# Dense 128-row projection of K, Q and attention outputs, with SBUF to SBUF moves between layouts, and norm products on GpSimd

## Chip, cores, metric

One core of a Trainium2 chip. The metric is device time in microseconds (us) from the first to the last instruction of one execution, as median over several executions. Ratios and their 95% intervals are computed from the mean time of one kernel's fast runs over the mean of the other's in the same rounds, so they are not quite the ratio of the medians that are quoted beside them.

## The reference

```python
# x: (1, 2048, 640) bf16, both branches read A_x; H = 32 heads of 20, D = 640
g = sigmoid((x * gate_w).sum(-1))                   # per token
a = full_attention(x, A_wqkv, A_wo)                 # softmax(q k^T / sqrt(20)) v, all 2048 keys
b = sliding_attention(x, B_wqkv, B_wo)              # 8 keys at distance 0, 2, ..., 14
out = g * a + (1 - g) * b                           # each branch through its own 640x640 output matrix
```

Branch A has 32 x 2048 x 2048 exponentials. That is over a million columns of 128 elements, and they decide the time of this kernel.

## The kernel before

The program is planned when it is built. A small scheduler in Python (`T(engine, duration, function, reads, writes)`) knows an estimated duration for each operation. It lets generators ("K projection", "Q projection", "B branch") compete for PSUM banks and for gaps on the engines, and writes out one fixed instruction order per engine, with the semaphore waits that the named buffers need. Every engine then works through its own list in order. An estimate that is wrong does not make the kernel wrong, only badly ordered. And any edit re-plans everything behind it, so small differences between two variants need not come from the edit itself.

The main loop works in tiles of two or three units. A unit is 128 keys x 512 queries of one head: a score matmul on TensorE (PE), an exponential on ScalarE (ACT), and a value matmul. A tile is three units wide only if the third bank of its score buffer is not lent to side work at that moment.

```python
# score buffers of three banks each; their third banks are lent to side work
score = [ps(1536, "score0"), ps(1536, "score1")]
BANKS = [(sbank, 0), (score[0], 1024), (score[1], 1024)]
# ... cut ...
def exp(s):                                   # one ScalarE instruction for 2 or 3 units
    exps[s] = T("act", actc(512 * n), lambda e: e.activation(
        ebuf[s % NE][:, 0:512 * n], score[s % 2][:, 0:512 * n], ACTF.Exp, scale=LN2 / STEP), ...)
```

Some units go to VectorE (DVE) instead: one operation from PSUM (`uD`), then, for a quad of four such units, five shifted integer operations (`eD`) whose sum in the value matmul approximates the exponential. The scheduler sends a quad this way whenever it sees VectorE idle.

Heads are handled in "quads": four heads of 20 rows, each padded to 32 partitions, so that four heads fill 128 partitions. Before the change every projection is made straight into this padded layout, which wastes 48 of 128 rows:

```python
def gen_k(q):                                 # 7 quads, 4 token chunks each (the first quad is made apart)
    T("dve", 0.36, w_pad(kvw, WKP_OFF, stage, 4 * DH * q, D, q), ...)        # pad the weights
    for tcc in range(4):
        b = yield from bank()
        # 5 matmuls into side[b]; then
        T("dve", dvc(512), ... kT[:, q, ...] = side[b] + onesrow ...)
        T("dve", dvc(512), ... tensor_reduce(kmx4, max, absolute) ...)       # bound for the softmax

def gen_q(g):                                 # one per group: (512 queries) x (quad)
    # 5 matmuls; qabs = |q| on DVE; a matmul with KM subtracts the bound; qT = scaled on DVE
    sl = g % 2                                # two Q buffers
# ... cut ...
def gen_norm(g):                              # after the last value matmul of a group
    T("dve", ... transpose(oTt, obank)); T("dve", ... reciprocal); T("dve", ... times gate)
    T("dve", dvc(512), lambda e: e.tensor_tensor(oo, ii, ib, ALU.mult), ...)
    T("dve", dvc(512), lambda e: e.transpose(oTn[:, sl, :], oNt), ...)
# ... cut ...
# output projection: 5 matmul groups of branch B and 8 of branch A (one per padded quad)
mms += [(side[b][:, 0:c1 - c0], oTn[:, (qc * NQ + q) % NSLOT, tok], woA_r[:, q, c0:c1]) for q in range(NQ)]
```

## Time and profile before

| | before |
|---|---|
| time, median of the first runs | 927.16 us (926.71 to 927.2) |
| span of the profiled execution | 924.7 us |
| ScalarE busy | 881.4 us, of it exponentials 863.5 |
| exponentials on ScalarE | 829 instructions, 1856 units |
| units on the VectorE path | 192 (48 quads) |

First some lines of the page. The first line gives for each engine its busy time, the share of the span and the number of instructions. Each digit of a row below is the busy share of one fortieth of the span in tenths; PEclk is the granted TensorE clock in tenths.

```profile
PE 905.5 (98%) x13935; PEld 322.1 (35%) x13938; DVE 697.6 (75%) x1209; ACT 881.4 (95%) x864; POOL 27.2 (3%) x23
...
ACT  6999999996999999999999999999999999999996
...
PEclk9999999998999999999999999999999999999999
```

ScalarE is full except for the head, the tail and one hole near 220 us, where the clock dips as well. PE's 98% does not mean that PE is the limit. The scheduler fills PE's gaps with dummy matmuls that keep the clock up: 392 groups of four, begun about 0.215 us apart where they follow each other in this trace.

The groups view with shapes kept apart shows: line, engine, operation, out<-in, shapes, count | busy us, mean ns of one | idle time before it, and what ended it.

```profile
L1239 ACT ACTIVATE ebuf<-score 128x1024 bf16<-128x1024 f32 x631 | 607.9, 1037 | 23.1 <-PE score L1216 20.0 <-ACT ebuf L1239 0.2
...
L1239 ACT ACTIVATE ebuf<-score 128x1536 bf16<-128x1536 f32 x198 | 282.4, 1469 | 3.9 <-PE score L1216 3.2
...
L594 DVE TENSOR_SCALAR eD<-uD 128x2048 int16<-128x2048 uint16 x240 | 164.1, 715 | 17.7 <-PE obank L1274 16.5
L1229 DVE TENSOR_SCALAR uD<-score 128x512 uint16<-128x512 f32 x192 | 131.7, 688 | 80.4 <-PE score L1216 79.2
...
L608 POOL COPY kvw<-stage 128x640 bf16<-128x640 bf16 x15 | 23.4, 1560 | 194.8 <-PE score L456 194.0
```

Two-unit exponentials dominate, 631 against 198. From the two mean times, a unit costs about 0.43 us and an instruction 0.17 us on top. But neighbouring instructions overlap (the two rows add up to more than the 863.5 us of the group without shapes): back to back, they start 0.92 and 1.34 us apart on average in this trace, which leaves about 0.08 us per instruction. So width is worth something.

The stage table gives for each stretch (us): its length, then busy time and instruction count of PE, PEld (weight loads), DVE, ACT and POOL (GpSimd), the granted clock, the DMA share and GB/s.

```profile
0.00:69.00 69.00, 65.58 (x861) 26.59 (x863) 43.27 (x100) 59.18 (x60) 3.79 (x8) 1.00 0.32 90
69.00:231.00 162.00, 155.78 (x2144) 48.05 (x2147) 131.87 (x217) 150.43 (x146) 23.40 (x15) 0.98 0.13 22
231.00:902.00 671.00, 666.10 (x10541) 239.41 (x10533) 516.60 (x883) 657.95 (x649) 0.00 (x0) 1.00 0.07 9
902.00:924.70 22.70, 18.09 (x401) 8.08 (x402) 5.92 (x10) 13.84 (x13) 0.00 (x0) 0.98 0.09 31
```

The number to subtract is ACT from the length: ScalarE idles 9.8, 11.6, 13.1 and 8.9 us in the four stages, 43.3 us in all.

Two single lines were used in the prediction. The first is the eD group between 200 and 232 us, while GpSimd copies B's weights. The second, from the listing of the tile WqP, gives the time that SyncE (SP) takes to issue a load: minimum/median/maximum in ns.

```profile
L594 DVE TENSOR_SCALAR eD<-uD 128x2048 int16<-128x2048 uint16 x10 | 13.6, 1398 | 1.2 <-PE obank L1274 1.2
```

```profile
L498 SPq DMA_DIRECT2D WqP<-in_A_wqkv_dram x150: 367/505/2952, 22.2 to 839.0; - x150
```

Last, GpSimd's two padding copies in the head, which the first K and Q projections wait for (timeline: start, duration):

```profile
5.67 0.52 POOL L425 COPY kvw<-repB 128x400 bf16<-128x400 bf16 x1 [2.30 <-DMA repB<-in_A_wqkv_dram]
8.01 0.53 POOL L425 COPY WqP<-repB 128x400 bf16<-128x400 bf16 x1 [1.83 <-DMA repB<-in_A_wqkv_dram]
```

### The profile page before, as it was taken

The numbers are of one execution on the slowest core, as the hardware profiler recorded it, in microseconds if no ns is written. First come the engines' busy times: TensorE is split into PE (matmuls) and PEld (weight loads), VectorE is DVE, ScalarE is ACT, GpSimd is POOL, SyncE is SP. The second block draws the span as 40 slices with busy tenths as digits, with TensorE's granted clock in tenths as the row PEclk, the third lists the DMA queues.
The fourth block names the chain that finished last, engine by engine and source line by source line (L and its number), as shares of the span: only waits on it lengthen the run. The fifth ranks groups of instructions, "written<-read, shape, count | busy, mean of one in ns | idle before, by whom it ended". The sixth has DMA issues, their size and how long they took to land.

```text
span 924.7 us, 31431 instructions
## 1 busy us (share of the span) xinstructions
PE 905.5 (98%) x13935; PEld 322.1 (35%) x13938; DVE 697.6 (75%) x1209; ACT 881.4 (95%) x864; POOL 27.2 (3%) x23
## 2 busy tenths in 40 slices
PE   8999999998999999999999999999999999999997
PEld 4333332322343333333433433433333343332333
DVE  6567778888888787988777877787786778678552
ACT  6999999996999999999999999999999999999996
POOL 1000000027000000000000000000000000000000
PEclk9999999998999999999999999999999999999999
DMA  6111000030000011001101001100001110000000
GB/s 194 25 50 16 6 3 7 6 113 6 3 7 6 7 14 14 3 6 14 15 6 14 10 7 14 14 7 7 3 7 13 21 14 7 2 6 7 2 2 30
DMA packets 89027, 16.27 MB, mean 18 GB/s; under 512 B 81596, under 2 KB 88252, under 8 KB 88892
## 3 DMA queue, kind: packets, MB, share of 16 engines
q1 hardware_dynamic: 88892, 14.27, 9.5%
q8 instruction: 110, 1.80, 0.8%
q14 instruction: 25, 0.20, 0.1%
HBM read 11.63 MB, written 2.62 MB: 15 GB/s over the span
## 4 chain that ended last, share of the span: by engine, by line
PE 82%; ACT 12%; DVE 2%; issue 2%; DVEq 0%; ACTq 0%
PE score L1216 25%; PE obank L1274 18%; PE score L456 16%; PE side L456 12%; ACT ebuf L1239 12%; PE side L1295 3%; PE obank L1295 3%; DVE eD L594 1%; PE score L1295 1%; PE score L669 1%; PE side L669 0%; PE obank L366 0%; PE score L945 0%; PE side L724 0%; PE score L724 0%
## 5 line engine op out<-in xcount | busy, mean ns | idle before, releaser
L1239 ACT ACTIVATE ebuf<-score 128x1024 bf16<-128x1024 f32 (+1 forms) x829 | 863.5, 1140 | 27.0 <-PE score L1216 23.2
L1216 PE MATMUL score<-qT,kT 32*128 32x512 bf16 x2048 | 332.5, 385 | 4.8 <-ACT ebuf L1239 2.4
L1229 DVE TENSOR_SCALAR uD<-score 128x512 uint16<-128x512 f32 x192 | 131.7, 688 | 80.4 <-PE score L1216 79.2
L1216 PEld LDWEIGHTS score<-qT,kT 32*128 32x128 bf16 x2048 | 80.0, 91 | 285.1 <-ACT ebuf L1239 143.6
L1274 PE MATMUL obank<-ebuf,vA 128*21 128x512 bf16 x1856 | 175.3, 386 | 3.8 <-DVE eD L594 2.8
L594 DVE TENSOR_SCALAR eD<-uD 128x2048 int16<-128x2048 uint16 x240 | 164.1, 715 | 17.7 <-PE obank L1274 16.5
L456 PE MATMUL score<-xT,kvw 128*32 128x256 bf16 (+1 forms) x1780 | 87.2, 299 | 0.8 <-ACT ebuf L1239 0.6
L1274 PE MATMUL obank<-eD,vA 128*21 128x512 bf16 x960 | 76.3, 380 | 0.0
L1274 PEld LDWEIGHTS obank<-ebuf,vA 128*21 128x21 bf16 x1856 | 43.1, 89 | 92.6 <-issue 68.2
L1295 PE MATMUL side<-xT,ident 128*32 128x512 bf16 x772 | 57.3, 382 | 0.0
L456 PE MATMUL side<-xT,kvw 128*32 128x256 bf16 (+1 forms) x1180 | 54.6, 289 | 0.2 <-DVE qT L519 0.2
L736 DVE TENSOR_TENSOR stage<-vB,repB 128x1280 bf16<-128x1280 bf16 x64 | 51.1, 816 | 0.3
L456 PEld LDWEIGHTS score<-xT,kvw 128*32 128x32 bf16 x1780 | 40.6, 95 | 30.4 <-issue 19.0
L659 DVE TENSOR_TENSOR stage<-qB,kB 128x1280 bf16<-128x1280 bf16 x64 | 50.1, 817 | 0.1
L1295 PE MATMUL obank<-xT,zero 128*32 128x512 bf16 x568 | 46.3, 384 | 0.0
L566 DVE STREAM_TRANSPOSE oTt<-obank 128x512 f32<-128x512 f32 x32 | 22.8, 714 | 16.1 <-PE obank L1274 15.9
L456 PEld LDWEIGHTS side<-xT,kvw 128*32 128x32 bf16 x1180 | 27.6, 96 | 17.3 <-issue 10.6
L1274 PEld LDWEIGHTS obank<-eD,vA 128*21 128x21 bf16 x960 | 23.8, 92 | 16.6 <-issue 1.9
L608 POOL COPY kvw<-stage 128x640 bf16<-128x640 bf16 x15 | 23.4, 1560 | 194.8 <-PE score L456 194.0
L456 PE MATMUL score<-xT,WqP 128*32 128x512 bf16 x300 | 25.0, 396 | 2.9 <-DVE uD L1229 2.9
L456 PE MATMUL side<-stage,ident 128*32 128x512 bf16 (+1 forms) x352 | 26.8, 372 | 0.0
L456 PE MATMUL score<-woA_r,oTn 128*32 128x128 bf16 (+1 forms) x568 | 26.7, 290 | 0.0
(165 smaller groups left out, 725.7 us busy)
## 6 DMA issues: line engine op xcount, KB each, us to landing
WqP<-in_A_wqkv_dram SPq DMA_DIRECT2D x150, 20.0 KB, 2.3
stage<-in_B_wqkv_dram SPq DMA_DIRECT2D x1, 2400.0 KB, 9.4
out_dram<-outsb SPq DMA_DIRECT2D x12, 160.0 KB, 1.8
oTn<-in_A_x_dram SPq DMA_DIRECT2D x2, 640.0 KB, 5.1
kvw<-in_A_wqkv_dram SPq DMA_DIRECT2D x1, 800.0 KB, 8.7
stage<-in_A_wqkv_dram SPq DMA_DIRECT2D x1, 800.0 KB, 9.8
woA_r<-in_A_wo_dram SPq DMA_DIRECT2D x4, 200.0 KB
woBp<-in_B_wo_dram SPq DMA_DIRECT2D x5, 160.0 KB
```

Source lines behind the costliest of these rows:

```text
L456: ins = e.matmul(o[32 * j:32 * j + 32, :], l[:, 32 * j:32 * j + 32], r, start=(first and i == 0), stop=(last and i == n - 1), skip_group_c ...
L566: T("dve", dvc(512), lambda e: e.transpose(oTt[:, :], obank[:, :]), reads=["obank"], writes=["oTt"])
L594: T("dve", 0.11 + 0.1334 * n, lambda e, k=k, sl=sl: e.tensor_scalar(eD[:, sl % NS, 0:512 * n].bitcast(I16), uD[d % 2][:, 0:512 * n], 0.25, ...
L608: T("pool", 2.2, lambda e, o=o, i=i: e.tensor_copy(o, i), reads=["stage"], writes=[("WkP", qq) for qq in range(NQ)] + ["WvA", ("wBp", m)])
L659: TB(dvc(CN * TOK, 2), lambda e, w=w, ks=ks: e.tensor_tensor(prodB(w), qB[:, :, :], ks, ALU.mult), reads=["qB", "kB"], writes=[("prod", w) ...
L669: ins = e.matmul(side[b][32 * w4:32 * w4 + 32, half * TOK:(half + 1) * TOK], Sel, pr, start=(half == 0 and f == 0), stop=(half == 1 and f ...
L736: TB(dvc(CN * TOK, 2), lambda e, w=w, vs=vs, rr=rr: e.tensor_tensor(prodB(w), vs, rr, ALU.mult), reads=["vB", ("repB", w4 % 2)], writes=[( ...
L1216: ins = e.matmul(o, kT[32 * j:32 * j + 32, q, kb * P:(kb + 1) * P], qT[g % 2][32 * j:32 * j + 32, :], start=True, stop=True)
L1229: t = T("dve", 0.69, lambda e: e.tensor_scalar(uD[d % 2][:, 512 * i:512 * (i + 1)], side[x], UOFF, 0.0, op0=ALU.add, op1=ALU.max), reads=[ ...
L1239: exps[s] = T("act", actc(512 * n), lambda e: e.activation(ebuf[s % NE][:, 0:512 * n], score[s % 2][:, 0:512 * n], ACTF.Exp, scale=LN2 / S ...
L1274: ins = e.matmul(obank[32 * j:32 * j + DV, :], vA[:, kb, GROUPS[g][1], j, :], src, start=(kb == 0), stop=(last and k >= len(lst) - 4), ski ...
L1295: ins = e.matmul(o[32 * j:32 * j + 32, :], w[:, 32 * j:32 * j + 32], xT[:, 0, 0:512], start=bool(best), stop=bool(best), skip_group_check= ...
```

## The change

Its intent: project K and Q in dense chunks of 128 rows (five chunks of 128 rows instead of eight padded quads), and project the output from five dense chunks instead of eight padded quads. This saves matmuls, PSUM bank uses and VectorE passes. The price is that pieces of up to 20 rows (one head) must be moved between the dense and the padded layout, by DMA from SBUF to SBUF. The products of the norm step go to GpSimd. B's work may no longer borrow the score buffers' third banks (`XPRIO` 9.0 to 3.5). The five loads of B's output weights move on SyncE's queue from the start (49 us) to behind the last K moves. The core of the diff, cut:

```diff
-    def gen_k(q):
-        ... pad, project, evacuate with +onesrow, maximum, for each quad and token chunk
+    def gen_kd():
+        for f in range(CN):
+            for tcc in range(4):
+                b = yield from bank()
+                ... 5 matmuls, 128 dense rows
+                i = next_dst()                       # one of three staging buffers, shared with Q
+                yield ("dve", DVE_AHEAD, sch.free(("dst", i)))
+                t = T("dve", dvc(512), ... tensor_copy(dst[i][0:m, :], side[b][0:m, :]) ...)
+                T("dve", dvc(512), ... tensor_reduce(kmd4 ...))
+                T("sp", 2.0 + 0.5 * len(pc), lambda e, ...: [e.dma_start(
+                    kT[32 * (h % 4) + 1 + r:32 * (h % 4) + 1 + r + n, h // 4, cols],
+                    dst[i][o:o + n, :]) for h, o, r, n in pc],       # one move per head piece
+                  ..., dma=True, nd=len(pc))
+    def gen_qd():                                    # 4 x 5 chunks instead of 32 groups
+        ... project, scale into dst[i], move the pieces to qT, |q|, bound matmul, qbnd, move the bounds
-    qT = [sb([P, 512], BF16, "qT%d" % i) for i in range(2)]
+    NQT = 4
+    qT = [sb([P, 512], BF16, "qT%d" % i) for i in range(NQT)]
+    for q in range(1, NQ):                           # new fills, ahead of the padding copies on GpSimd
+        T("pool", 0.95, lambda e, q=q: e.tensor_copy(kT[:, q, :].bitcast(FP32), ones ...), writes=[("kTz", q)])
     def gen_norm(g):
-        T("dve", ... tensor_tensor(oo, ii, ib, ALU.mult) ...)
+        en, c1, c2 = ("dve", 0.12, dvc(512)) if g == NG - 1 else ("pool", 0.25, 1.3)
+        T(en, c2, ... tensor_tensor(oo, ii, ib, ALU.mult) ...)
+        T("sp", 2.0 + 0.5 * len(pc), ... oTd[dense rows] <- oN[1][padded rows] ..., dma=True, nd=len(pc))
-    mms += [... oTn, woA_r ... for q in range(NQ)]   # 8
+    mms += [... oTd, woA_d ... for f in range(CN)]   # 5
     # scheduler: a DMA task now occupies its queue for iss * nd
-            self.avail[stream] = start + 0.06
+            self.avail[stream] = start + iss * nd    # iss = 0.5 unless given
-    XPRIO = 9.0
+    XPRIO = 3.5
```

## The prediction

> **What bounds it now.** ScalarE. The page shows ACT busy 881 of 924.7 us (95%), 863.5 of it the softmax exponentials: 631 of 1024 columns (1037 ns) and 198 of 1536 (1469 ns). That is 0.43 us per 512-column unit plus about 0.09 us per instruction; 1856 of 2048 units go here. From 231 to 902 us (stage table) ACT is 98% busy, so the exponentials' busy time must fall. ACT also idles 8.3 us between 208 and 231 us. The chain of waits names PE (82%), but it includes 392 groups of four filler matmuls (0.215 us each, 84 us): PE has slack.
>
> VectorE (75% busy) decides how much ACT is spared: 48 quads (192 units) take the VectorE path, each costing 4x0.688 + 5x0.715 = 6.3 us of VectorE and 0.86 us of extra PE; it spares ACT about 1.8 us.
>
> **What the change removes** (groups view).
> - VectorE: K evacuation and maxima 28 -> 20 tiles, -13 us; Q work of 31 groups (52 us) become 20 chunks of about 1.65 us plus one padded group, -18; norm product and its small multiply move to GpSimd, -27; padding, clears, -4. Together about -60 us.
> - PE, at 0.215 us per group: K -9, Q -8, output projection (13 -> 10 terms) -13: -30 us.
> - PSUM: K and Q use the banks less, and B's work and the output projection no longer borrow the exponentials' third score banks. So more exponentials cover three units: I expect some 700 instructions, not 829.
>
> **What it adds.** About 500 small SBUF to SBUF DMAs, issue about 0.5 us and landing about 2 us, estimated from the WqP loads here (0.505 and 2.3 us). Q is prepared up to three groups ahead, so this should be hidden. GpSimd gains 31 products (estimated 1.3 us) and about 10 us of clears and fills before its head padding copies.
>
> GpSimd's cost falls on VectorE: the Trainium skill, "SBUF — State Buffer", Two separate sides, calls the shared port pair an exclusive lock. The trace agrees: while GpSimd copies B's weights from 202.5 to 226.8 us, eD operations average 1.40 us, not 0.69, and ACT loses 8 us. After, these copies come in three bursts (I expect 3 us lost, not 8), but 31 products add stalls of up to about 1 us on VectorE, half of what they free.
>
> **Sum on ACT, the critical path.** Freed VectorE time nets about 40 us after port stalls and lower utilisation: six to eight more quads, -12 us. About 130 fewer instructions at 0.09: -11. Weight-copy stall: -5. Head: the padding copies, ending at 8.5 us now, start after about 12: +3. New waits, late DMAs, port stalls: +2. Total -23: **904 us**, range 888 to 921. Chances: faster by over 2% 0.64, within 2% 0.31, slower 0.05.
>
> **What would show it.** Exponentials near 700 with most three units wide; VectorE-path units 192 -> about 220; exponentials' busy 863 -> about 840; no 8 us hole near 208 us; first exponential later than 20.95 us; eD and B products occasionally over 1.3 us beside GpSimd products.
>
> **What would make it wrong.** If B's work, left with one PSUM bank, falls behind, it is forced at the end and the tail grows. If Q or K pieces land late, score matmuls wait on DMA. If port stalls eat most of the freed VectorE time, quads do not rise and the gain is only instruction overhead (about 915).

## The result, and the profile after

| | before | after |
|---|---|---|
| time, median | 926.93 us (926.54 to 927.2) | 957.45 us (955.55 to 960.45) |
| ratio, 95% interval | | 1.0333 (1.03 to 1.0365) |
| span of the profiled execution | 924.7 us | 957.4 us |
| exponentials on ScalarE | 829, 863.5 us busy | 725, 843.5 us busy |
| units on the VectorE path | 192 | 228 |
| ScalarE idle | 43.3 us | 98.8 us |

The change is 3.3% slower. The page of the kernel after:

```profile
PE 892.0 (93%) x13790; PEld 327.6 (34%) x13790; DVE 697.5 (73%) x1177; ACT 858.6 (90%) x759; POOL 79.7 (8%) x98
...
ACT  3997775699899889979999899999999999999995
...
PEclk8998977799999999999999999999999999999999
```

ScalarE has less to do, as intended, but holes between the third and the ninth slice, and the granted clock falls there too. The groups (columns as before):

```profile
L1371 ACT ACTIVATE ebuf<-score 128x1536 bf16<-128x1536 f32 x370 | 517.0, 1474 | 19.5 <-PE score L1348 18.4
L1371 ACT ACTIVATE ebuf<-score 128x1024 bf16<-128x1024 f32 x355 | 348.8, 1038 | 52.7 <-PE score L1348 50.7
...
L716 DVE TENSOR_SCALAR eD<-uD 128x2048 int16<-128x2048 uint16 x285 | 194.2, 710 | 13.1 <-PE obank L1406 12.0 <-DVE eD L716 0.2
...
L1361 DVE TENSOR_SCALAR uD<-score 128x512 uint16<-128x512 f32 x228 | 154.7, 687 | 88.6 <-PE score L1348 87.5
```

ScalarE's expected savings are there: 57 quads on VectorE instead of 48, and half of the exponentials three units wide. But ScalarE now stands idle before the exponentials for 72 us, not 27; 69 us of it, not 23, are put down to scores. The stage table shows where:

```profile
0.00:69.00 69.00, 61.19 (x806) 26.52 (x810) 37.11 (x90) 51.10 (x54) 16.79 (x26) 0.95 0.41 125
69.00:231.00 162.00, 141.56 (x1812) 45.33 (x1804) 103.08 (x165) 123.36 (x115) 25.39 (x21) 0.86 0.12 29
231.00:902.00 671.00, 639.38 (x10372) 237.91 (x10372) 523.13 (x872) 640.21 (x556) 36.28 (x50) 0.99 0.06 15
902.00:957.40 55.40, 49.84 (x819) 17.89 (x811) 34.18 (x52) 43.90 (x37) 1.27 (x2) 1.00 0.05 16
```

Subtracting as before, ScalarE idles 17.9 (+8.1), 38.6 (+27.0), 30.8 (+17.7) and 11.5 (+2.6) us: 55 us of new idle time, against 23 us less busy time.

What stands behind the second stage is seen in the chain of work that ended last, followed back from the last instruction to its releasers. Here is a stretch of it (start, duration, what):

```profile
130.53 0.61 SPq L537
131.18 0.74 SPq L537
131.97 0.72 SPq L537
```

This is SyncE's queue issuing K moves, one after the other; between 118 and 150 us line 537 makes up 63% of the chain. From 69 to 231 us it is 21%, and the Q moves (line 598) are another 9%; before the change SyncE is not among the lines that lead this stretch of the chain. The timeline of the queue itself over the same time shows no gap (start, time over all of the group, count):

```profile
118.65 28.15 SPq L537 DMA_DIRECT2D kT<-dst x38
146.92 0.44 SPq L556 DMA_DIRECT2D WqP<-in_A_wqkv_dram x1
147.41 5.98 SPq L598 DMA_DIRECT2D qT<-dst x8
153.50 2.98 SPq L701 DMA_DIRECT2D oTd<-oN x4
```

The listings of the lines give the time to issue one (ns, minimum/median/maximum): K pieces, Q pieces, Q bounds, output pieces, and the loads of whole Q weight chunks for comparison.

```profile
L537 SPq DMA_DIRECT2D kT<-dst x128: 554/707/1277, 39.1 to 177.7; - x128
L598 SPq DMA_DIRECT2D qT<-dst x136: 555/717/1567, 74.2 to 846.9; - x136
L631 SPq DMA_DIRECT2D qT<-qbnd x42: 521/556/829, 85.4 to 852.1; - x42
L701 SPq DMA_DIRECT2D oTd<-oN x140: 554/718/1128, 68.6 to 928.9; - x140
L556 SPq DMA_DIRECT2D WqP<-in_A_wqkv_dram x24: 374/390/522, 28.6 to 814.3; - x24
```

There are 446 moves. With the 0.04 us between two of them, a piece takes about 0.75 us of the queue, where both the prediction and the scheduler had counted 0.5. From 39 to 231 us the groups of the queue's timeline add up to 168 of 192 us, for 202 issues. Not all of that is the price of issuing: added up singly, the issues take 140 us, about 150 with the short pauses between them. Most of the rest are the five loads of B's output weights, which take about 0.54 us each to issue but hold the queue for 17.9 us, because each waits for the one before to land. (Before the change they held it for 18.6 us, from 49 us, and ScalarE was still busy for 45.2 of the 46 us from 23 to 69 us.) The queue is in order: a Q move stands behind the K moves issued before it, VectorE then waits for a staging buffer (16.9 us on K moves in the list of waits), PE waits for VectorE, and ScalarE for scores. A PE that waits can also lose its clock. The Trainium skill, "TensorE: Matmul & The Clock Gate", Part 1, says that the array falls to half its clock after an idle window and needs sustained work to come back. The trace agrees: after PE's 3.59 us of waiting in the head (below), the granted clock from 13 to 16 us is 0.50. From 69 to 231 us its mean is 0.86, not 0.98.

Lastly the head. GpSimd's timeline: the seven new fills stand ahead of the padding copies.

```profile
5.79 6.93 POOL L414 COPY kT<-ones 128x1024 f32<-128x1024 f32 x7 [0.77 <-DVE offs L418]
12.66 0.52 POOL L460 COPY kvw<-repB 128x400 bf16<-128x400 bf16 x1
13.12 0.52 POOL L460 COPY WqP<-repB 128x400 bf16<-128x400 bf16 x1
```

The weights have long landed, but the copies are done 5 us later than before. The first exponential starts at 27.36 us, not 20.95.

### The profile page after: what moved, and what is told of

Its sections match the earlier page's. It is cut to its first block, busy times and chain, and to the rows that moved or that the text cites. A ratio compares the mean times of both kernels' runs of the same rounds, so it can differ in the third digit from the quotient of the medians.

```text
span 957.4 us, 31402 instructions
## 1 busy us (share of the span) xinstructions
PE 892.0 (93%) x13790; PEld 327.6 (34%) x13790; DVE 697.5 (73%) x1177; ACT 858.6 (90%) x759; POOL 79.7 (8%) x98
## 4 chain that ended last, share of the span: by engine, by line
PE 64%; ACT 16%; DVE 7%; SPq 6%; issue 5%; DMA 1%; POOL 1%; DVEq 0%; ACTq 0%; POOLq 0%
PE score L1348 17%; PE side L493 16%; ACT ebuf L1371 15%; PE obank L1406 15%; PE obank L1427 4%; PE score L1427 4%; PE score L493 4%; SPq L537 4%; DVE eD L716 2%; SPq L598 2%; DVE uD L1361 1%; POOL kT L414 1%; DVE stage L780 1%; PE side L847 1%; PE side L793 1%
## 5 line engine op out<-in xcount | busy, mean ns | idle before, releaser
L1371 ACT ACTIVATE ebuf<-score 128x1024 bf16<-128x1024 f32 (+1 forms) x725 | 843.5, 1260 | 72.2 <-PE score L1348 69.1
L1348 PE MATMUL score<-qT,kT 32*128 32x512 bf16 x2048 | 294.8, 392 | 24.6 <-ACT ebuf L1371 14.9
L716 DVE TENSOR_SCALAR eD<-uD 128x2048 int16<-128x2048 uint16 x285 | 194.2, 710 | 13.1 <-PE obank L1406 12.0
L493 PE MATMUL side<-xT,kvw 128*32 128x256 bf16 (+1 forms) x2510 | 106.0, 284 | 3.2 <-DVE vB L764 1.2
L1427 PE MATMUL obank<-xT,zero 128*32 128x512 bf16 x1012 | 82.9, 384 | 0.0
L1427 PE MATMUL score<-xT,ident 128*32 128x512 bf16 x984 | 80.7, 382 | 0.1
L493 PEld LDWEIGHTS side<-xT,kvw 128*32 128x32 bf16 x2510 | 61.7, 97 | 39.8 <-issue 18.4
L696 POOL TENSOR_TENSOR oN<-oTt,rcp 128x512 bf16<-128x512 f32 x31 | 35.8, 1155 | 2.4
L493 PE MATMUL side<-woBp,oB 128*32 128x128 bf16 (+1 forms) x600 | 30.4, 311 | 4.4 <-DMA oTd<-oN 4.2
L1427 PEld LDWEIGHTS score<-xT,ident 128*32 128x32 bf16 x984 | 23.5, 95 | 29.2 <-ACT ebuf L1371 13.4
L493 PE MATMUL score<-xT,kvw 128*32 128x512 bf16 (+1 forms) x250 | 25.0, 417 | 7.6 <-DVE dst L529 7.6
```

Of the source, the lines that this page charges most:

```text
L493: ins = e.matmul(o[j:k, :], l[:, j:k], r, start=(first and i == 0), stop=(last and i == n - 1), skip_group_check=True)
L696: T(en, c2, lambda e: e.tensor_tensor(oo, ii, ib, ALU.mult), reads=["rcp", "oTt"], writes=["oN0"])
L716: T("dve", 0.11 + 0.1334 * n, lambda e, k=k, sl=sl: e.tensor_scalar(eD[:, sl % NS, 0:512 * n].bitcast(I16), uD[d % 2][:, 0:512 * n], 0.25, ...
L1348: ins = e.matmul(o, kT[32 * j:32 * j + 32, q, kb * P:(kb + 1) * P], qT[g % NQT][32 * j:32 * j + 32, :], start=True, stop=True)
L1371: exps[s] = T("act", actc(512 * n), lambda e: e.activation(ebuf[s % NE][:, 0:512 * n], score[s % 2][:, 0:512 * n], ACTF.Exp, scale=LN2 / S ...
L1427: ins = e.matmul(o[32 * j:32 * j + 32, :], w[:, 32 * j:32 * j + 32] if best else w[:, :], xT[:, 0, 0:512], start=bool(best), stop=bool(bes ...
```

## The experiments

Theory A: the moves fill SyncE's queue; the number of issues at 0.75 us is what costs. Rivals: B, the ring of three staging buffers is too shallow, or landing latency hurts. C, the queue would have had room, but the fixed order was planned with 0.5 us. G, GpSimd's products hold a port that VectorE needs. Separately: the head is late because of the order of GpSimd's list. "The changed kernel" below is the kernel after (957.45 us). Runs without a remark gave the right result. One rival runs through all of them: every edit makes a new plan, and no run separates its worth from the edit's own. e_iss, which changes only what the planner believes, moved the time by 12.7 us. So a gain of that size is put down to a cause only where the profile also shows that cause's own trace: the start of the first exponential, the waits, the queue's time.

### The fills behind the padding copies (e_head)

```diff
-    for q in range(1, NQ): T("pool", 0.95, ... fill kT[:, q] ...)      # ahead of the two w_pad tasks
+    ... the same loop right behind the two w_pad tasks
```

> Edit: the seven GpSimd fills of kT are placed behind the two padding copies that the first K and Q projections wait for; nothing else. If the head loses its time because the padding copies queue behind the fills (they end at 13.6 us in the changed kernel, 8.5 us before), the first exponential comes back from 27.4 us to about 21 us and the whole is 5 to 7 us shorter, near 951 us. If the late head has another cause (slower loads of x, the SyncE queue), the first exponential stays past 25 us and the time stays within 2 us of the changed kernel.

Measured: 944.58 us (941.28 to 948.05), ratio to before 1.0192 (1.0164 to 1.022). The first exponential starts at 20.66 us. The cause of the late head is shown. The gain of 12.9 us is about twice what the head explains (6.7 us). Where the other 6 us came from was not isolated; the whole order behind the head was planned anew. The stage table puts 7.4 us less idle time of ScalarE into the third stage, and none into the second.

### Deeper staging, the same number of moves (e_kring)

Two buffers of 2048 columns for K, in memory that is idle at that time (woBp and oB), the moves unchanged.

```diff
-                i = next_dst(); ... dst[i][0:m, :] ...
+                i = f % 2; kd = _ap(kds[i], tcc * 512, [[1, 512]]) ... kd[0:m, :] ...     # kds = [woBp, oB]
```

> Control: K chunks are staged in two buffers of 2048 columns (memory idle at that time) instead of sharing three buffers of 512 columns with Q; still 128 K moves of 512 columns. Theory A (SyncE needs about 0.75 us to issue each piece move and its queue is full from 39 to 231 us): the queue stays full, so the time changes by less than 8 us (950 to 960 us). Theory B (the ring of staging buffers is too shallow, or landing latency is what hurts): the waits of VectorE on K moves vanish and most of the loss between 69 and 231 us returns, 15 to 27 us, near 935 us.

Measured: 946.51 us (941.11 to 948.24), ratio 1.0199 (1.0162 to 1.0236): 10.9 us better, between the two forecasts, so each of them missed. VectorE's waits on K moves are gone from its list of waits, but the queue is as full as before (142 us of issues, added singly, between 39 and 231 us, where the changed kernel has 140). The second stage:

```profile
69.00:231.00 162.00, 146.64 (x2028) 49.08 (x2017) 112.82 (x183) 136.67 (x130) 26.37 (x23) 0.93 0.12 29
```

ScalarE idles 25.3 us in it instead of 38.6. So depth is a real part of the loss in this stage.

### The same staging, K moved once per piece (e_kmerge)

```diff
+                if tcc % 4 != 3:
+                    continue
+                kd = _ap(kds[i], 0, [[1, 2048]])          # one move of 2048 columns per head piece
```

> Same staging buffers as the control, but each K piece is moved once with 2048 columns: 32 K moves, not 128, the same bytes. Theory A (issue count on SyncE): 96 issues of 0.75 us, 72 us of queue time, go; ScalarE's idle time between 69 and 231 us falls from about 40 us to under 15, the granted clock there returns near 1.0, and the time is 20 to 30 us shorter than the changed kernel, 928 to 940 us. Theory B (depth of the ring): no better than the control. If issue time grows with the bytes of a row instead of being fixed per move (over 2 us each), no gain either.

Measured: 933.96 us (928.65 to 935.85), ratio 1.0068 (1.0035 to 1.01): 23.5 us better than the changed kernel and 12.5 us better than the control with the same memory. The listing of the K moves of one of the two buffers, and the second stage:

```profile
L543 SPq DMA_DIRECT2D kT<-woBp x18: 600/717/858, 59.3 to 154.9; - x18
```

```profile
69.00:231.00 162.00, 147.85 (x2171) 51.32 (x2163) 123.58 (x200) 144.75 (x136) 27.58 (x23) 0.97 0.13 30
```

A move of four times the bytes is issued in the same 0.72 us: the price is per move, not per byte. ScalarE idles 17.3 us in this stage instead of 38.6 (slightly more than the 15 expected), the clock is back at 0.97, and the queue's issues, added singly, take 77 us instead of 140. This is what theory A expected of the time. But against the control, with 25.3 us, the smaller number of moves took 8 us off ScalarE's idle time in this stage, where depth had taken 13.3: count and depth both cost, and which is the larger is not shown.

### The same moves, planned at 0.75 us (e_iss)

```diff
-                T("sp", 2.0 + 0.5 * len(pc), ..., dma=True, nd=len(pc))
+                T("sp", 2.0 + 0.75 * len(pc), ..., dma=True, nd=len(pc), iss=0.75)       # K, Q, outputs
```

> Only the planner's belief is changed: piece moves of K, Q and outputs are planned at 0.75 us of SyncE time each and not 0.5; the moves themselves stay. Theory C (the queue would have had room, the fixed instruction order was laid for a queue that is half again too fast, so in-order engines stand still): 15 us or more come back, 935 to 942 us. Theory A in its strict form (capacity: the queue is full whatever the order): under 8 us come back.

Measured: 944.75 us (942.42 to 947.39), ratio 1.0194 (1.017 to 1.0218): 12.7 us better with not one move fewer. Both forecasts missed it, in between. So a part of the loss is the plan's wrong belief. The second and third stage show where:

```profile
69.00:231.00 162.00, 130.67 (x1695) 41.13 (x1691) 99.58 (x164) 121.29 (x119) 24.31 (x21) 0.87 0.12 29
231.00:902.00 671.00, 648.98 (x10667) 243.34 (x10664) 525.18 (x867) 655.37 (x564) 36.48 (x50) 1.00 0.06 15
```

ScalarE idles 40.7 us in the second stage (38.6 in the changed kernel) and 15.6 in the third (30.8). A truer price left the crowded stage as it was; the gain came behind it. ScalarE's longest wait is now 13.6 us, at 200 us, right behind the five loads of B's output weights, which hold the queue for 18.8 us; the run with mended loads (v1w) below looks at that.

### The norm products back on VectorE (e_norm_back)

```diff
-        en, c1, c2 = ("dve", 0.12, dvc(512)) if g == NG - 1 else ("pool", 0.25, 1.3)
+        en, c1, c2 = ("dve", 0.12, dvc(512))
```

> One part of the change undone: all 32 norm products run on VectorE again, everything else as changed. Theory G (GpSimd products hold the port that VectorE needs and so cost the time): the time falls by 8 us or more. Theory A (SyncE's queue and the head): VectorE gets about 27 us of work back, so some three quads fewer take its path, ScalarE works about 5 us more, and the time stays within 6 us of the changed kernel (951 to 964 us).

Measured: 962.48 us (957.53 to 964.68), ratio 1.0377 (1.0346 to 1.0408): no gain, 5 us slower if anything. Theory G falls. The groups say the same: eD took 710 ns on average in the changed kernel and 715 before; the products of B rose only from 817 to 836.

### Three mends together (v1)

e_head + e_kmerge + e_iss.

> Three mends together: the fills behind the padding copies, K pieces moved once with 2048 columns, and the remaining piece moves planned at 0.75 us. Each alone gave 12.5, 23 and 12.5 us; they share causes, so I expect not the sum of 48 but 30 to 38 us: 919 to 928 us, about level with the kernel before. If the causes were independent: 910 us.

Measured: 914.76 us (913.11 to 915.81), ratio 0.9873 (0.9857 to 0.9889). The gain is 42.7 us, more than the 30 to 38 expected and close to the sum of the three (49). The changed kernel is now faster than the one before, by 1.3%.

### B's output weights without waits on each other (v1w)

The five loads fill different parts of one tile but shared one dependency name, so each waited for the one before to land.

```diff
-            T("sp", 6.0, ... woBp[:, dp, :] ..., writes=["woBp"], dma=True, iss=3.7)
+            T("sp", 6.0, ... woBp[:, dp, :] ..., writes=[("woBp", dp)], dma=True, iss=0.55)
```

> As v1, and the five loads of B's output weights no longer wait for one another (each filled its own part of the tile but shared one dependency name), so they hold SyncE's queue for about 3 us and not 18. If a blocked queue is what delays Q (the changed planning alone had one 13.6 us hole of ScalarE right behind these loads), 3 to 8 us better than v1; if not, within 3 us of it.

Measured: 911.6 us (910.74 to 912.77), ratio 0.9836 (0.9821 to 0.9851): 3.2 us better than v1, at the lower edge of the expected range. The loads now hold the queue for 3.3 us, not 18.7. But ScalarE's idle time in the second stage did not fall (7.1 us, 5.8 in v1), so a blocked queue as the cause is not shown; a difference of this size could also come from the new plan alone.

### Output moves issued by GpSimd (v1w_pool)

```diff
-            T("sp", 2.0 + 0.75 * len(pc), ... oTd ... <- oN[1] ...)
+            T("pool", 2.0 + 0.75 * len(pc), ... oTd ... <- oN[1] ...)
```

> As v1w, and the 140 moves of attention outputs are issued by GpSimd's queue, about 100 us of issue time off SyncE. If SyncE's queue still delays Q and the output projection (waits of scores for the Q bound, of the projection for outputs), 3 to 10 us better than v1w. If GpSimd takes longer per move or its products queue behind its own moves, worse than v1w.

Measured: 906.72 us (904.62 to 907.63), ratio 0.9779 (0.9764 to 0.9795): 4.9 us better than v1w, and 2.2% faster than before. Its second stage and the listing of the output moves on GpSimd's queue:

```profile
69.00:231.00 162.00, 153.35 (x2319) 54.95 (x2320) 129.66 (x216) 154.85 (x147) 38.98 (x50) 1.00 0.13 29
```

```profile
L704 POOL DMA_DIRECT2D oTd<-oN x140: 502/514/1848, 60.3 to 872.9; - x140
```

ScalarE idles 7.1 us in the second stage, less than before the change, and the clock is 1.00. PE's waits for DMA are down to 1.8 us in all. The Trainium skill, "DMA: Bandwidth & Descriptors", Issuing engines are not separate DMA queues, says that starting DMAs on several engines "will only save the time on the sequencer it takes to initiate the DMA, which is usually small relative to the DMA itself." The first half fits what helped here. The second does not: SyncE took 0.72 us to issue an output piece, and on GpSimd's queue the same pieces land in 1.8 us (median).

### 128 K moves again, in the mended kernel (v2_k128)

The edit is e_kmerge's, undone in v1w_pool (the staging memory stays).

> The mended kernel with output moves on GpSimd's queue (906.7 us), but K again in 128 moves of 512 columns (same staging memory). Theory A: SyncE must issue 96 more moves of 0.75 us, 72 us more between 40 and 210 us, so ScalarE loses time there again: 5 to 20 us slower, 912 to 927 us. If the earlier gain of merging came only from the order of planning, within 4 us of 906.7.

Measured: 913.13 us (911.77 to 915.64), ratio 0.9858 (0.9838 to 0.9878): 6.4 us slower, within what theory A expected, with a plan that knew the price. ScalarE idles 11.7 us in the second stage, not 7.1. So the count of issues seems to cost by itself, not only through a wrong price in the plan, though a part of 6.4 us can be the new order. It costs less here than in the changed kernel (12.5 us between e_kring and e_kmerge); that the queue has been relieved elsewhere would explain it, and was not tested.

### The norm products on VectorE, in the mended kernel (v2_norm)

> The mended kernel with the norm products back on VectorE: the worth of moving them to GpSimd where SyncE does not spoil it. VectorE gets 27 us of work back, three or four quads fewer take its path (55 to about 51), ScalarE works 5 to 8 us more: 910 to 916 us. If GpSimd's hold of the shared port eats the gain, within 2 us of 906.7 or faster.

Measured: 915.33 us (914.95 to 916.33), ratio 0.988 (0.9866 to 0.9895). There are 204 units on the VectorE path, not 220, and the exponentials keep ScalarE busy for 848.7 us, not 841.4. So with SyncE's queue relieved, moving the products to GpSimd is worth 8.6 us here, most of it in ScalarE's work.

### Five Q buffers (v2_q5)

```diff
-    NQT = 4
-    ND = 3
+    NQT = 5
+    ND = 2
```

> The mended kernel with five Q buffers and two staging buffers instead of four and three, so Q may be prepared one group earlier. If scores still wait for late Q (1.8 us of waits for the Q bound are left in the profile), 0 to 4 us faster; I expect no difference beyond 3 us.

Measured: 902.48 us (901.27 to 906.19), ratio to before 0.9736 (0.9719 to 0.9752): 4.2 us better than v1w_pool, a little more than expected. This is the best kernel, 2.6% faster than before and 5.7% faster than the changed kernel. Whether it is the earlier Q or the new plan was not separated.

### Third score banks lent to B again (v2_x9, e_x9)

```diff
-    XPRIO = 3.5
+    XPRIO = 9.0
```

In the mended kernel:

> The mended kernel, but B's work and the output projection may again borrow the third score banks. My prediction gave these banks about 11 us: fewer of the exponentials should then be three units wide, about 780 to 820 instructions and not 726, and the time 4 to 10 us longer (911 to 917 us). If B's work on one bank holds things up instead, it gets faster.

Measured: 912.37 us (912.09 to 912.45), but the result was wrong (relative error 0.44). To see whose fault that was, the same number was put back in the changed kernel alone:

> The changed kernel with one number put back: B's work and the output projection may borrow the exponentials' third score banks, as before. If the new bank rule gives the exponentials their width, their count rises from 725 to about 800 to 830, as in the wrong-result run of the mended kernel (817), and ScalarE works 6 to 8 us more; the time stays within 8 us of 957 because SyncE's queue sets it (950 to 966 us). If B's starving on one bank cost time, over 8 us faster. If its result is wrong too, the fault comes with the bank rule of the changed kernel; if it is right, with one of my mends.

Measured: 970.02 us (967.74 to 975.0), slower than expected, and again a wrong result (relative error 0.54). So it does not come with the mends: the changed kernel does not bear this setting. Why is open. Their times are therefore not evidence about a right kernel. What the profiles of both show is the width: 817 and 821 exponentials instead of 727 and 725. This agrees with the prediction's view of the bank rule: for some 90 to 96 instructions more, the exponentials' busy time is 9.8 and 11.4 us longer (with slightly different numbers of units).

## Why the prediction was wrong

It forecast 904 us and 2.5% faster; measured were 957.45 us and 3.3% slower. Point by point:

- **The work taken off ScalarE: right.** The exponentials' busy time fell by 20.0 us (forecast 23), the instructions to 725 (forecast some 700, "most three units wide": 370 of 725 were), and nine quads more went to VectorE (forecast six to eight). That the total fits is in part luck. An estimate: 36 units fewer at 0.43 us are 15.5 us, where the prediction had 12, which leaves 4.5 us for 104 fewer instructions, where it had 11.
- **"issue about 0.5 us and landing about 2 us, estimated from the WqP loads here (0.505 and 2.3 us). Q is prepared up to three groups ahead, so this should be hidden": this step failed.** The price was taken from loads of another shape. A piece from SBUF to SBUF costs about 0.75 us of the queue. Worse, the price was never multiplied by the count in the stage where most moves fall. Even at 0.5 us the 202 issues between 39 and 231 us come to 101 us (an estimate from the count); measured, they took about 150 of 192 us, and the waits of B's weight loads on each other some 15 more, in an in-order queue that also carries the Q pieces for which the scores wait. So Q was not hidden: "New waits, late DMAs, port stalls: +2" in the sum should have been over 40, the +27.0 and +17.7 us of idle ScalarE in the second and third stage. In the second stage the chain runs through the queue, and deeper staging and fewer issues (e_kring, e_kmerge) gave back 21.3 of the 27.0 us. In the third the chain touches the queue only in a few short stretches; a plan with the right price (e_iss) gave back 15.2 of the 17.7 us there. How the loss divides between count, depth and plan stays open. v1w_pool ends at 906.7 us, close to the forecast. This fits a sum that was otherwise about right, but does not prove it, since the mends also took away the head's delay and the wait of the weight loads.
- **The head, "+3": mechanism right, size wrong.** The first exponential came 6.4 us late. The padding copies started behind the fills at 12.7 us, as forecast ("after about 12"). What was left out is that PE, idle meanwhile, runs slower afterwards: the five matmuls of the first K projection took 2.31 us, where the five of the next one took 1.24. The granted clock was 0.50 from 13 to 16 us.
- **GpSimd's port: too pessimistic for the products, too hopeful for the copies.** "half of what they free" was not seen: with 31 of the 32 products on GpSimd the mean eD operation took 710 ns. In the mended kernel it took 702 ns with the products on GpSimd and 688 without, an estimated 4 us over 275 operations, and the move was worth 8.6 us. But the weight copies, forecast to lose 3 us in three bursts, ran ten in a row from 173.7 to 189.4 us; from 173 to 196 us ScalarE idles 7.1 us, though SyncE's queue has a share in this.
- **The warning list named it.** "If Q or K pieces land late, score matmuls wait on DMA" was written down as a risk and given no number. The first on that list, B's work forced at the end, did not come: ScalarE's idle time in the last stage grew by only 2.6 us.

## What to carry to other kernels

A change that trades compute for many small moves has a budget of its own: issues times price per issue, per stage, on the one queue that issues them, held against the length of that stage. Take the price from a trace of moves of the same kind, and look for critical data that stands in the same in-order queue. Here fewer and longer moves, deeper staging, a second issuing engine, a plan that knows the price, and mends of the head's order and of one row of weight loads turned 3.3% slower into 2.6% faster, without touching the idea of the change. When each edit makes a new plan, look for the cause's own mark in the profile before you give it the time.

## What the Trainium skill lacked or had wrong

- "DMA: Bandwidth & Descriptors", Issuing engines are not separate DMA queues: issue time is called usually small relative to the DMA. Here an SBUF to SBUF move of up to 20 rows took 0.72 us of SyncE to issue (GpSimd-issued ones landed in 1.8 us), and 202 issues took about 150 of the queue's 192 us from 39 to 231 us.
- No page that I found gives what it costs SyncE to issue one move by shape. The runs show medians of 0.71 to 0.72 us for pieces of up to 20 rows, with rows of 1 KB and of 4 KB alike, 0.56 for the Q bounds of one to four rows, and 0.39 for a weight load of 128 partitions.
- "DMA: Bandwidth & Descriptors", Issuing engine by pattern, calls DMAs through sync or scalar generally faster, and does not say in what. The issue alone was not faster: for these pieces the trace shows 0.51 us (median; 0.62 mean) per issue on GpSimd and 0.72 on SyncE, with the reserve that spans on GpSimd are rough in this profile; moving 140 of them there gained 4.9 us.
- "SBUF — State Buffer", Two separate sides: its exclusive port agrees with the trace (eD at 1.40 us on average beside back-to-back GpSimd copies), but the page gives no measure for sparse GpSimd work: with 31 products spread over the kernel, eD stayed at 0.71 us.
